# A long convolution's complex product by three real products in eight small tiles, and a new order of the operations ahead of the feed-forward loop

## The chip, the core and the metric

The kernel runs on one core of a Trainium2 chip. The core has five engines with a queue each: TensorE (PE, with its weight loads PEld), VectorE (DVE), ScalarE (ACT), GpSimd (POOL) and SyncE (SP), which here issues all DMAs. Each engine works through its instructions in the order of the program. The metric is the device time of one execution in microseconds, the median over the runs shown.

## The reference, cut to what matters

```python
x = A_q                                           # 1 x 2048 x 512
sa, ca, ga, sb, cb, gb = split(silu(c) @ w_mod)   # six vectors of 512
h = layernorm(x) * (1 + ca) + sa
kv = short_conv(k, shift_k) * v                   # 4 taps, causal, per channel
y = irfft(rfft(pad(kv)) * rfft(pad(ssm_k)))[:2048] + kv * ssm_D
x = x + ga * (h * y)
h = layernorm(x) * (1 + cb) + sb
x = x + gb * ((silu(h @ w_gate) * (h @ w_up)) @ w_down)   # 512 -> 1792 -> 512
```

Everything is float32. The long convolution has 2048 positions for each of 512 channels and is causal.

## The kernel before, in words

The kernel has a front part (modulation, short convolution, long convolution, first norm, gate, residual) and a feed-forward part over 28 sets, a set being one block of 128 of the 1792 hidden channels for one half of the 2048 rows. Here "row block" t = 0 to 3 is 512 rows; the first half of the sets works on row blocks 0 and 1.

**The long convolution** is a Fourier transform in two steps, done by matmuls, for four blocks `c_` of 128 channels. For the data: `load_k`, `load_v` (lines 115, 120), the taps on DVE (`tap0`, `tap`, lines 133, 141), the product with v (`times_v`, line 147), PE transposes (`x_turn`, line 167, tile `kvt`) and the first step (`x_first`, line 175, tile `s`, into `X[c_]`). For the kernel: `load_ssm` (line 723), `skip` (line 727, adds `ssm_D`), first step (`k_first`, line 195, also tile `s`), transposes back (`k_turn`, line 213, tile `kt`, into `K[c_]`). DVE then transposes 32x32 blocks of a quarter of `X[c_]`, a piece of 32 channels (`swap_x`, line 232, `STREAM_TRANSPOSE`).

The second step works on one piece n of 16. `second` (line 251) multiplies the 64 rows of the two halves `a` by a 64x64 matrix; its two column halves go to two halves of PSUM's partitions, so a call is four matmuls in the four 64x64 tiles of the array, 512 columns each. `x2nd` (line 262) does this for the data (tile `px`) and ACT copies the result to `xs`. `product` (line 266) does it twice for the kernel (tile `pk`), with the matrices `W2` and `W2S`, and DVE multiplies each with `xs` into `R`: four real products of real and imaginary parts, as two of doubled height. `inv` (line 275) goes back with `V1` and `V2` (tile `iv`), eight matmuls in 64x64 tiles, and ACT copies into `X`. `loop` (line 285) runs the pieces: `product(n)`, `x2nd(n + 1)`, `swap_x(n + 2)`, the hooks of n, `inv(n - 1)`, the hooks of `(n,)`. The other work of the front is hung on the hooks (from line 801 on): taps and first steps of later blocks, modulation (`mod_load`, `mod_part`, `mod_bc`, tiles `wm`, `pb`, `bcs`), loads, statistics (`do_stats`), gates (`do_gate`, `gate`, line 394: four ACT steps and two POOL steps for each row block).

The result of blocks 0 to 2 is put to DRAM and got back in another order (`put`, `get`, lines 238, 242, one and four DMAs); block 3 is swapped again by DVE. `y_pe` (line 403, tile `y`) does the last step, `y_gate` (line 415) multiplies with the gate `S1`, `add_c` and `add_y` (lines 795, 425) add to `xt`, with the statistics of the second norm (`bnb`, `mvb`, `rsb`).

**The feed-forward part** splits each float32 operand into a high and a low part in a reduced float32 type, and takes three matmuls for a product (`op_hi`, `op_lo`, `split_w`, `w8_hi`, `w8_lo`). Sets 0 and 1 are done plainly (`gu_pe`, line 621, tile `g`, 96 matmuls in all), sets 2 to 27 by `gate_up` (line 658), with seven products in the order 1, 5, 7, 2, 3, 6, 4 in place of eight. `split_w` (line 533) needs four sums and two low parts on POOL for each set. `downs` multiplies back (tile `dn`). Behind each product stands a place where more work is hung (`AT`, line 962): among it `norm2b` and `half_t` (lines 436, 470), the second norm and PE transposes (tile `nt`) of row blocks 2 and 3.

**What sets the order.** Every engine keeps the program's order, which is written out: first a list (lines 731 to 777), then `loop` with its hooks, then a list to the second set (lines 834 to 928), then the loop over sets. Tiles come from pools: `e8` has 8 buffers of 8 KB for each partition, `b16` 6 of 16 KB, `r4` 5 of 4 KB, PSUM in the front four double banks (`banks`). A tile is given out when an old one of its pool is no longer read.

Of the kernel before, what the change touches and what calls it, by code (L numbers as in the profile page):

```python
# [10 lines left out]
F32 = mybir.dt.float32  # L11
# [32 lines left out]
def adaln_h3_swiglu(ctx, tc, q, kT, vT, shk, ssm, dskip, wgu, wdn, c, wmod, e_fwd, e_inv, w_c, out):  # L44
# [122 lines left out]
    def x_turn(c_, half):  # L167

        pt = banks("kvt").rearrange("p a (j d) -> p (a j) d", j=4)
        for jj in range(8):  # L170
            pe.transpose(pt[:, jj], U[c_][:, 8 * half + jj :: J], ident)
        x = XT[c_, half] = r4([P, 8, P], F32, f"x{c_}{half}")
        act.copy(x, pt)
# [74 lines left out]
    xs, R = {}, {}  # L248
    PIECES = 4 * NB
# [16 lines left out]
    def product(n):

        R[n] = []
        for w in (W2, W2S):
            ps = second(w, K[n // 4], n % 4, "pk")  # L270
            r = r4([P, 2, 512], F32, "R")
            dve.tensor_tensor(r, ps, xs[n], op=ALU.mult)
            R[n].append(r)

    def inv(n):
        ps = banks("iv")
        for k, v in enumerate((V1, V2)):
            for a in range(2):
                for c_ in range(2):
                    pe.matmul(  # L280
                        ps[rows(a), c_, :], v[rows(c_)], R[n][k][rows(c_), a, :], start=(k == 0), stop=(k == 1)
                    )
        act.copy(piece(X[n // 4], n % 4), ps.rearrange("p g (k d) -> p (g k) d", k=16))

    def loop(hooks):
        for n in range(PIECES + 1):
            if n < PIECES:
                product(n)
            if n + 1 < PIECES:
                x2nd(n + 1)  # L290
            if n + 2 < PIECES:
                swap_x(n + 2)
            for f in hooks.get(n, ()):
                f()
            if n > 0:
                inv(n - 1)
            for f in hooks.get((n,), ()):
                f()
# [432 lines left out]
    load_k(0)  # L731
    load_e(0)
    load_e(1)
    load_ssm(0)
    load_e(2)
    load_e(3)
    load_v(0)
    load_k(1)
    load_v(1)
    wc = cp.tile([P, 4, 64], F32, name="wc")  # L740
    sp.dma_start(wc, w_c)
    W2, W2S, V1, V2 = (wc[:, i, :] for i in range(4))
    def kf(c_, *jqs):
        return [lambda jq=jq: k_first(c_, jq) for jq in jqs]

    def kt(c_, *ms):
        return [lambda m=m: k_turn(c_, m) for m in ms]

    def run(fs):
        for f in fs:  # L750
            f()

    tap0(0, dve)
    tap(0, 1)
    load_ssm(1)
    skip(0)
    run(kf(0, 0, 1, 2, 3))
    tap(0, 2)
    tap(0, 3)
    times_v(0, dve)  # L760
    x_turn(0, 0)
    x_turn(0, 1)
    x_first(0, 0)
    run(kt(0, 0, 1))
    x_first(0, 1)
    run(kt(0, 2, 3))
    tap0(1, dve)
    for t in range(1, KS):
        tap(1, t)
    load_k(2)  # L770
    swap_x(0)
    swap_x(1)
    x2nd(0)
    times_v(1, dve)
    load_v(2)
    tap0(2, act)
    skip(1)
# [17 lines left out]
    def add_c(t, *cs):
# [50 lines left out]
    rs = {0: norm2a(0, True)}
    w8_lo(0, pool)
    add_c(1, 0)
    y_now(1, 2, 3)
    mod_T(3)  # L850
    mod_T(4)
    y_pe(2, 0, 1)
    y_pe(3, 0, 1)
    y_pe(2, 2, 3)
    norm2b(0, rs[0], 0)
    norm2b(0, rs[0], 1)
    add_c(1, 1)
    norm_t(0, 0)
    norm_s(0, 0)
    y_gate(2, 0, 1)  # L860
    y_gate(3, 0, 1)
    add_y(2, 0, 4, (0, 1), pool)
# [204 lines left out]
```

## Time and profile before

| | before |
|---|---|
| median of 3 runs | 643.6 us (643.42 to 643.73) |
| the profiled execution | 643.63 us, span 641.9 us |
| PE, DVE, ACT, POOL busy | 601.9, 472.3, 299.5, 315.5 us |
| mean granted PE clock | 0.984 |
| first matmul of the feed-forward part | at 194.05 us |

All operations of the kernel are recorded through one helper, so they have one line (L40) in the profile, and groups are told apart by their tiles: `out<-in`, the program's names without buffer numbers. A group's row has engine, operation, tiles, shapes and count, then busy us, mean ns of one, and after the second bar the idle time ahead of it with what ended it. In order of time a row has start, length, engine, operation, count, and in brackets the idle time before it. Matmuls overlap, so the cost of a row of them is read from one start to the next.

### The profile page before, as it was taken

How to read it: one execution, taken by the hardware profiler on the slowest of the kernel's cores; microseconds unless marked ns; L12 is line 12 of the kernel's file. 1: busy time of each engine (PE TensorE's matmuls, PEld its weight loads, DVE VectorE, ACT ScalarE, POOL GpSimd, SP SyncE). 2: the span in 40 equal slices, each digit the busy share in tenths (PEclk: the TensorE clock that was granted, in tenths of full speed). 3: DMA queues.
4: the chain of work that ended last, by engine and by line, in shares of the span. 5: the costliest groups of instructions: out<-in, count | busy, mean ns of one | idle time of the engine just before them, and what ended most of it. 6: DMA issues, size and time to landing. Idle time of an engine off the chain costs nothing.

```text
span 641.9 us, 9081 instructions
## 1 busy us (share of the span) xinstructions
PE 601.9 (94%) x3604; PEld 454.8 (71%) x3604; DVE 472.3 (74%) x600; ACT 299.5 (47%) x439; POOL 315.5 (49%) x248
## 2 busy tenths in 40 slices
PE   2899999989697899999999999999999999999997
PEld 2756456534276788777778888878888888888885
DVE  5998767957978688877766886898565665656655
ACT  1867667874124545454544443544343333333320
POOL 0000000599254479775673767486565757575400
PEclk9999999989889999999999999999999999999999
DMA  8884492953931121302022111114210112120003
GB/s 293 370 300 161 165 234 86 269 103 137 242 115 66 34 67 33 99 33 67 20 79 66 34 34 65 34 66 154 75 67 34 65 38 86 43 65 1 0 2 131
DMA packets 30107, 64.68 MB, mean 101 GB/s; under 512 B 2289, under 2 KB 14705, under 8 KB 27506
## 3 DMA queue, kind: packets, MB, share of 16 engines
q1 hardware_dynamic: 30066, 64.11, 31.7%
q8 instruction: 28, 0.46, 0.3%
q14 instruction: 13, 0.11, 0.1%
HBM read 53.62 MB, written 10.49 MB: 100 GB/s over the span
## 4 chain that ended last, share of the span: by engine, by line
PE 54%; DVE 16%; ACT 5%; issue 2%; POOL 1%; ACTq 0%; DVEq 0%; POOLq 0%
PE dn L40 19%; PE b L40 9%; PE a L40 8%; PE c L40 8%; PE d L40 5%; DVE d L40 2%; DVE x L40 2%; PE y L40 2%; DVE acts L40 2%; DVE n L40 1%; DVE X L40 1%; ACT acts L40 1%; ACT op L40 1%; PE pk L40 1%; DVE c L40 1%
## 5 line engine op out<-in xcount | busy, mean ns | idle before, releaser
L40 PE MATMUL dn<-wd,acts 128*128 128x512 f32 x672 | 165.9, 390 | 0.5 <-DVE acts L40 0.5
L40 PEld LDWEIGHTS dn<-wd,acts 128*128 128x128 f32 x672 | 126.0, 188 | 27.9 <-DVE acts L40 1.1
L40 POOL TENSOR_TENSOR wa<-ws,wa 128x512 fp32r<-128x512 f32 (+1 forms) x52 | 60.6, 1188 | 110.9 <-ACT wa L40 103.1
L40 DVE TENSOR_TENSOR x<-x,dn 128x512 f32<-128x512 f32 x112 | 74.6, 680 | 54.4 <-PE dn L40 53.3
L40 PE MATMUL b<-op,wsum 128*128 128x512 f32 x312 | 79.7, 391 | 0.8 <-POOL wsum L40 0.8
L40 POOL TENSOR_TENSOR wsum<-sr,wsum 128x1024 fp32r<-128x1024 f32 x26 | 72.3, 2779 | 0.0
L40 PEld LDWEIGHTS b<-op,wsum 128*128 128x128 f32 x312 | 58.1, 188 | 13.3 <-POOL wsum L40 1.3
L40 POOL TENSOR_SCALAR rsa<-mva 128x4 f32<-128x4 f32 x8 | 2.5, 310 | 118.5 <-DVE mva L40 118.0
L40 PE MATMUL a<-op,wa 128*128 128x512 f32 x228 | 57.9, 389 | 0.0
L40 ACT ACTIVATE sg<-sg 128x512 f32<-128x512 f32 x26 | 16.5, 633 | 87.4 <-DVE sg L40 87.4
L40 DVE TENSOR_TENSOR R<-pk,xs 128x1024 f32<-128x1024 f32 x32 | 37.7, 1215 | 25.2 <-PE pk L40 25.2
L40 PEld LDWEIGHTS a<-op,wa 128*128 128x128 f32 x228 | 42.8, 188 | 8.9
L40 DVE STREAM_TRANSPOSE X<-X 128x1024 f32<-128x1024 f32 x20 | 45.3, 2277 | 0.1
L40 POOL TENSOR_TENSOR wd<-wds,wd 128x1024 fp32r<-128x1024 f32 x14 | 35.5, 2538 | 19.6 <-ACT wd L40 19.6
L40 ACT CAST acts<-d 128x512 fp32r<-128x512 f32 x26 | 15.3, 587 | 62.9 <-DVE d L40 36.5
L40 POOL TENSOR_TENSOR sr<-ws 128x256 f32<-128x256 f32 x52 | 43.1, 828 | 0.0
L40 PE MATMUL c<-op,wa 128*128 128x512 f32 x156 | 39.7, 390 | 0.0
L40 PE MATMUL d<-op,wsum 128*128 128x512 f32 x156 | 39.6, 389 | 0.0
L40 PE MATMUL c<-op,wsum 128*128 128x512 f32 x156 | 39.6, 389 | 0.0
L40 POOL TENSOR_TENSOR s<-s,bcs 128x2048 f32<-128x2048 f32 x8 | 36.5, 4568 | 0.3
L40 PE MATMUL pk<-K,wc 64*64 64x512 f32 x256 | 35.3, 626 | 1.1 <-ACT K L40 1.0
L40 DVE TENSOR_TENSOR op<-hraw,op 128x1024 fp32r<-128x1024 f32 x14 | 23.1, 1654 | 15.2 <-ACT op L40 15.2
(105 smaller groups left out, 1095.9 us busy)
## 6 DMA issues: line engine op xcount, KB each, us to landing
ws<-in_wgu SPq DMA_DIRECT2D x28, 512.0 KB, 3.3
wds<-in_wdn SPq DMA_DIRECT2D x14, 512.0 KB, 3.6
wm<-in_wmod SPq DMA_DIRECT2D x6, 1024.0 KB, 11.4
away<-X SPq DMA_DIRECT2D x3, 2048.0 KB, 7.5
X<-away SPq DMA_DIRECT2D x12, 512.0 KB, 11.2
kt<-in_kT SPq DMA_DIRECT2D x4, 1024.0 KB, 5.4
ss<-in_ssm SPq DMA_DIRECT2D x4, 1024.0 KB, 10.0
vt<-in_vT SPq DMA_DIRECT2D x4, 1024.0 KB, 10.1
```

The source lines that it names most:

```text
L40: return lambda *a, **k: self.tc.keep_in_program_order(f(*a, **k))
```

## The change

Three things change.

*The complex product.* Three real products are taken in place of four. `second` now takes pieces two at a time (64 channels; n runs over 8) and one of three 64x32 matrices m, and issues eight matmuls in 64x32 tiles. `x3` does the data side (three times for a pair of pieces, copied by ACT), `product3` the kernel side and DVE's product, in place. `inv3` goes back with three 32x64 matrices in 32x64 tiles: 24 matmuls into two PSUM tiles. The constants are made to fit.

*The order.* `loop` and its hooks are gone. One written list holds all operations from the first load to the end of sets 0 and 1. Steps are cut finer for it: the loads of block 0's `ssm` in quarters, `times_v` in four parts, the gate's ACT and POOL steps apart (`gate_n`, `gate_p`), statistics in halves. Four groups of six `warm` matmuls on an identity stand in it (before: one of four). The norm and transposes of row block 1 now stand ahead of the first `gu_pe`.

*Inside the loop over sets,* `half_t` moves from behind product 2 to behind product 3, and one `norm_stats` from 3 to 2.

```diff
-    def second(w, t, i, name):
+    def groups():
+        for i in range(2):
+            for c_ in range(2):
+                for a in range(2):
+                    yield i, c_, a, slice(64 * i + 32 * c_, 64 * i + 32 * c_ + 32)
+
+    def second(w, t, n, m, name):
         ps = banks(name)
-        for c_ in range(2):
-            for a in range(2):
-                pe.matmul(
-                    ps[rows(c_), a, :], w[rows(a)], piece(t, i)[rows(a), 16 * c_ : 16 * c_ + 16], start=True, stop=True
-                )
+        for i, c_, a, r in groups():
+            x = piece(t, 2 * (n % 2) + i)[rows(a), 16 * c_ : 16 * c_ + 16]
+            pe.matmul(ps[r, a, :], w[rows(a), m], x, start=True, stop=True)
         return ps
...
+    def x3(n, m):
+        if m == 0:
+            t = fp.tile([P, 2, 512], F32, tag="xs", name="xs", bufs=2)
+        else:
+            t = r4([P, 2, 512], F32, "xs")
+        xs[n, m] = t
+        act.copy(t, second(WX, X[n // 2], n, m, "px"))
+
+    def product3(n, m):
+        t = xs[n, m]
+        dve.tensor_tensor(t, second(WK, K[n // 2], n, m, "pk"), t, op=ALU.mult)
+
+    def inv3(n):
+        ps = [banks("iv") for _ in range(2)]
+        for m in range(3):
+            for i, c_, a, r in groups():
+                pe.matmul(ps[i][rows(a), c_, :], WV[r, m], xs[n, m][r, a, :], start=(m == 0), stop=(m == 2))
+        for i in range(2):
+            act.copy(piece(X[n // 2], 2 * (n % 2) + i), ps[i].rearrange("p g (k d) -> p (g k) d", k=16))
...
-    loop({
-        0: [lambda: tap(2, 1), lambda: load_ssm(2), lambda: x_turn(1, 0)],
...
-    })
...
+    load_k(0)
+    tap0(0, dve)
+    tap(0, 1)
+    load_ssm(0, 0)
+    load_ssm(0, 2)
+    load_ssm(0, 3)
+    warm(6)
+    load_e(2)
+    skip(0)
+    warm(6)
+    load_e(0)
+    k_first(0, 2)
...
+    x3(0, 0)
+    x3(0, 1)
+    mod_load(0, 5)
+    x3(0, 2)
+    product3(0, 0)
+    tap(2, 2)
+    x_first(1, 0)
+    load_ssm(3)
+    x3(1, 0)
+    load_x(0)
+    product3(0, 1)
+    x3(1, 1)
+    product3(0, 2)
+    product3(1, 0)
+    product3(1, 1)
+    k_turn(1, 2)
+    tap(2, 3)
...
+    x3(5, 0)
+    gate_p(0)
...
+    get(1)
+    product3(5, 2)
+    inv3(4)
+    inv3(5)
+    swap_x(13)
...
+    y_pe(0, 0, 1)
     load_w(0)
+    y_gate(0, 0, 1)
...
+    put(2)
+    mod_load(3, 4)
+    y_pe(2, 0, 1)
...
+    inv3(7)
+    w8_hi(0)
+    mod_part(4)
+    swap_x(14)
+    warm(6)
+    swap_x(15)
+    mod_part(3)
+    get(2)
+    y_pe(0, 2)
     load_w(1)
     load_wd(0)
...
+    norm_t(1, 1)
+    load_w(2)
     room()
+    op_lo("B21")
+    norm_s(1, 1)
+    gu_pe(1, 0, 0)
...
-        (5, 2): lambda: half_t(2, 0),
+        (5, 3): lambda: half_t(2, 0),
...
-        (6, 2): lambda: half_t(2, 1),
-        (6, 3): lambda: norm_stats(3, range(0, 2)),
+        (6, 3): lambda: half_t(2, 1),
+        (6, 2): lambda: norm_stats(3, range(0, 2)),
...
-        (7, 2): lambda: half_t(3, 0),
+        (7, 3): lambda: half_t(3, 0),
...
-        (8, 2): lambda: half_t(3, 1),
+        (8, 3): lambda: half_t(3, 1),
...
+    re, im = np.concatenate([co, -si]), np.concatenate([si, co])
+    w_k = np.concatenate([re, im - re, re + im], 1)
+    w_x = np.concatenate([re + im, re, im], 1)
+    w_v = np.concatenate([co + si, co - si, si, co, -co, si], 1)
```

More of the change, by code (lines that the diff above doesn't have):

```diff
@@ L170, in x_turn @@
         for jj in range(8):
-            pe.transpose(pt[:, jj], U[c_][:, 8 * half + jj :: J], ident)
+            pe.transpose(pt[:, jj], kv[c_][1][:, 8 * half + jj :: J], ident)
         x = XT[c_, half] = r4([P, 8, P], F32, f"x{c_}{half}")
@@ L266, in product @@
[L266 to L298, printed above, removed]
+    xs = {}
+    def groups():
+        for i in range(2):
+            for c_ in range(2):
+                for a in range(2):
+                    yield i, c_, a, slice(64 * i + 32 * c_, 64 * i + 32 * c_ + 32)
@@ L729, in skip, with load_wc @@
         dve.tensor_tensor(t, t, dsk[:, c_ * P : (c_ + 1) * P], op=ALU.add)
[L731 to L777, printed above, removed]
+    wc = cp.tile([P, 384], F32, name="wc")
+    WK, WX = (wc[:, 96 * i : 96 * i + 96].rearrange("p (m k) -> p m k", m=3) for i in range(2))
+    WV = wc[:, 192:].rearrange("p (m k) -> p m k", m=3)
+    def load_wc():
+        sp.dma_start(wc, w_c)
     def mod_mix():
@@ new lines, in adaln_h3_swiglu @@
+    tap(0, 2)
+    load_v(0)
+    k_first(0, 0)
+    load_e(3)
+    load_e(1)
+    k_first(0, 3)
+    load_ssm(0, 1)
+    load_k(1)
+    load_v(1)
+    k_first(0, 1)
+    load_k(2)
+    tap(0, 3)
+    times_v(0, 0)
+    times_v(0, 1)
+    x_turn(0, 0)
+    load_ssm(1)
+    load_wc()
+    k_turn(0, 0)
+    k_turn(0, 1)
+    times_v(0, 3)
+    mod_load(1, 2)
+    times_v(0, 2)
+    x_turn(0, 1)
+    k_turn(0, 2)
+    tap0(1, dve)
+    k_turn(0, 3)
+    tap(1, 1)
+    tap(1, 2)
+    tap(1, 3)
+    times_v(1, 0)
@@ new lines, in adaln_h3_swiglu @@
+    x_first(0, 0)
+    x_first(0, 1)
+    skip(1)
+    k_first(1, 3)
+    k_first(1, 2)
+    k_first(1, 0)
+    times_v(1, 1)
+    k_first(1, 1)
+    times_v(1, 3)
+    times_v(1, 2)
+    x_turn(1, 1)
+    mod_part(1)
+    swap_x(1)
+    swap_x(0)
+    k_turn(1, 0)
+    x_turn(1, 0)
+    k_turn(1, 3)
+    swap_x(2)
+    load_k(3)
+    load_v(2)
+    mod_bc(1)
+    swap_x(3)
+    tap0(2, act)
+    mod_part(2)
+    load_ssm(2)
+    tap(2, 1)
+    x3(0, 0)
+    x3(0, 1)
+    mod_load(0, 5)
+    x3(0, 2)
@@ new lines, in adaln_h3_swiglu @@
+    product3(0, 0)
[11 more added lines that the diff above has]
+    tap(2, 3)
+    k_turn(1, 1)
+    skip(3)
+    x3(1, 2)
+    x_first(1, 1)
+    do_stats(0, 0)
+    tap0(3, act)
+    product3(1, 2)
+    inv3(0)
+    times_v(2, 0)
+    times_v(2, 1)
+    inv3(1)
+    x_turn(2, 0)
+    times_v(2, 2)
+    times_v(2, 3)
+    x_turn(2, 1)
+    skip(2)
@@ new lines, in adaln_h3_swiglu @@
+    load_v(3)
+    k_first(2, 0)
+    k_first(2, 1)
+    tap(3, 1)
+    put(0)
+    swap_x(5)
+    swap_x(4)
+    k_first(2, 3)
+    swap_x(7)
+    mod_part(0)
+    k_first(2, 2)
+    x_first(2, 0)
+    x_first(2, 1)
+    tap(3, 2)
+    tap(3, 3)
+    times_v(3, 0)
+    k_turn(2, 0)
+    k_turn(2, 2)
+    k_turn(2, 1)
+    times_v(3, 2)
+    swap_x(6)
+    times_v(3, 1)
+    mod_bc(2)
+    x3(2, 0)
+    times_v(3, 3)
+    x3(2, 1)
+    product3(2, 0)
+    load_x(1)
+    load_x(2)
+    x3(2, 2)
@@ new lines, in adaln_h3_swiglu @@
+    product3(2, 1)
+    product3(2, 2)
+    x3(3, 0)
+    mod_bc(0)
+    do_stats(0, 1)
+    product3(3, 0)
+    load_x(3)
+    x3(3, 1)
+    product3(3, 1)
+    do_stats(3, 0)
+    x3(3, 2)
+    product3(3, 2)
+    gate_n(0, 0)
+    x_turn(3, 1)
+    gate_n(0, 1)
+    inv3(2)
+    swap_x(11)
+    swap_x(9)
+    get(0)
+    inv3(3)
+    put(1)
+    mod_part(5)
+    k_turn(2, 3)
+    x_turn(3, 0)
+    mod_bc(5)
+    swap_x(8)
+    do_stats(2, 0)
+    k_first(3, 1)
+    mod_mix()
+    k_first(3, 2)
@@ new lines, in adaln_h3_swiglu @@
+    swap_x(10)
+    k_first(3, 3)
+    k_first(3, 0)
+    do_stats(1, 0)
+    x3(4, 0)
+    product3(4, 0)
+    x3(4, 1)
+    x_first(3, 0)
+    x_first(3, 1)
+    x3(4, 2)
+    x3(5, 0)
+    gate_p(0)
+    do_stats(1, 1)
+    do_stats(2, 1)
+    x3(5, 1)
+    x3(5, 2)
+    do_stats(3, 1)
+    gate_n(1, 0)
+    gate_n(2, 0)
+    swap_x(14)
+    load_einv()
+    product3(4, 1)
+    product3(4, 2)
+    product3(5, 0)
+    product3(5, 1)
+    gate_n(1, 1)
+    gate_n(2, 1)
+    get(1)
+    product3(5, 2)
@@ new lines, in adaln_h3_swiglu @@
+    inv3(4)
+    inv3(5)
+    swap_x(13)
+    k_turn(3, 0)
+    k_turn(3, 3)
+    swap_x(15)
+    swap_x(12)
+    gate_n(3, 0)
+    y_pe(0, 0, 1)
+    load_w(0)
+    y_gate(0, 0, 1)
+    k_turn(3, 1)
+    add_c(0, 0)
+    add_c(0, 1)
+    k_turn(3, 2)
+    x3(6, 0)
+    x3(6, 1)
+    x3(6, 2)
+    gate_p(1)
+    product3(6, 0)
+    product3(6, 1)
+    product3(6, 2)
+    y_pe(1, 0, 1)
+    y_gate(1, 0, 1)
+    add_c(1, 0)
+    x3(7, 0)
+    add_c(1, 1)
+    inv3(6)
+    x3(7, 1)
+    gate_n(3, 1)
@@ L845, in adaln_h3_swiglu @@
+    y_gate(0, 3)
     add_c(0, 3)
[L846 to L849, printed above, removed]
+    w8_hi(1)
+    y_pe(1, 2, 3)
+    do_norm2a(0)
+    mod_T(4)
+    y_gate(1, 2, 3)
+    add_c(1, 2)
     mod_T(3)
[L851 to L852 removed]
     y_pe(3, 0, 1)
[L854 removed]
+    norm2b(0, rs[0], 1)
+    warm(6)
     norm2b(0, rs[0], 0)
[L856 to L857 removed]
     norm_t(0, 0)
     norm_s(0, 0)
[L860 to L862 removed]
```

233 lines of the change are left out of this document (112 added, 121 removed).

## The prediction

> **What bounds the kernel now.** I read the page first, then the busy time by stretches, then what DVE and PE waited for, and last the instructions in order of time. The page's head, slices and chain:
>
> ```profile
> span 641.9 us, 9081 instructions
> ...
> PE   2899999989697899999999999999999999999997
> ...
> PEclk9999999989889999999999999999999999999999
> ...
> PE 54%; DVE 16%; ACT 5%; issue 2%; POOL 1%; ACTq 0%; DVEq 0%; POOLq 0%
> ```
>
> The profiled execution took 643.63 us for a span of 641.9, so 1.7 lie around the span; the median shown is 643.6, the same. From slice 14 on PE is full at full clock. Before it the bound changes, as the busy time by stretches shows (columns: PE, PEld, DVE, ACT, POOL, clock, DMA share, GB/s):
>
> ```profile
> 7.67:57.72 50.05, 42.63 (x462) 30.26 (x463) 48.39 (x35) 32.14 (x40) 0.00 (x0) 1.00 0.84 330
> 57.72:112.75 55.03, 54.02 (x508) 29.16 (x506) 39.91 (x38) 38.36 (x46) 0.00 (x0) 1.00 0.55 148
> ...
> 7.67:194.05 186.38, 168.29 (x1688) 98.93 (x1688) 152.34 (x166) 112.31 (x139) 52.72 (x31) 0.95 0.68 207
> 194.05:216.51 22.46, 17.13 (x78) 13.71 (x76) 17.40 (x25) 12.19 (x17) 7.65 (x7) 0.92 0.17 59
> 216.51:641.90 425.39, 416.44 (x1841) 342.19 (x1841) 301.50 (x403) 173.48 (x283) 254.48 (x205) 1.00 0.17 55
> ```
>
> 7.67 is DVE's first tap, 194.05 the first matmul of the feed-forward part (`g`). To 57.72 DVE is full, then to 112.75 PE is. Over 7.67 to 194.05 DVE stands idle 34.0 us (186.38 - 152.34), mostly for `pk`:
>
> ```profile
> DVE R L40 <- PE pk L40: 25.2, 11, 6.6
> ```
>
> One turn of the loop in the middle stretch, in order of time:
>
> ```profile
> 74.55 1.95 PE L40 MATMUL pk<-K,wc 64*64 64x512 f32 x16
> 76.32 1.04 PE L40 MATMUL px<-X,wc 64*64 64x512 f32 x8
> 77.28 1.98 PE L40 MATMUL pb<-part,sel 128*128 128x512 f32 x4
> 79.20 1.95 PE L40 MATMUL iv<-R,wc 64*64 64x512 f32 x16
> 81.08 2.06 PE L40 MATMUL s<-x,er 64*128 64x128 f32 x32
> 83.06 1.06 PE L40 MATMUL pb<-wm,csb 128*32 128x512 f32 x8
> 84.06 1.95 PE L40 MATMUL pk<-K,wc 64*64 64x512 f32 x16
> ```
>
> PE has no gap in these 9.51 us; DVE waits because the next `pk` stands behind work of other blocks. So a stretch full on DVE is followed by one full on PE: what order and amount of the work cost is read here.
>
> **The cut.** Everything from the first `g` on I take as one block. Before, it is 641.9 - 194.05 = 447.9 us. Its own losses: 51 `g` matmuls took 22.46 us up to 216.51. A group of six takes 1.36 us by the starts below, so 51 need 11.6: 10.9 lost. One wait for POOL costs 259.19 - 256.82 - 1.36 = 1.0, and four waits for `n` cost 4.0:
>
> ```profile
> PE nt L40 <- DVE n L40: 4.0, 4, 1.2
> ```
>
> ```profile
> 255.46 1.52 PE L40 MATMUL c<-op,wa 128*128 128x512 f32 x6
> 256.82 1.52 PE L40 MATMUL a<-op,wa 128*128 128x512 f32 x6
> 259.19 1.66 PE L40 MATMUL b<-op,wsum 128*128 128x512 f32 x6 [0.84 <-POOL wsum L40]
> ```
>
> Without them the block is 432.0 us.
>
> **half_t one product later** (behind 3, not 2). Each time PE reaches the transposes 0.8 to 1.2 us before `n` is there; one product ahead of them is 1.36 us. Gain 4.0, bounds 0 and 4.0; I take 3.9. `hraw`'s copies come 1.36 later, and their reader is sets away.
>
> **The first sets in the new order.** Both row blocks are now normalised before the first `g`, and 96 `g` (21.8 us) and four downs (24 matmuls, 5.4) stand in one row. Of the 10.9 I take all as gone, since it was PE waiting on `op`, `n` and `sg` inside the group. What could bring it back is POOL, which has from the first weight split to the sums of the fifth set (f = 4):
>
> ```profile
> L40 POOL TENSOR_TENSOR s<-s,bcs 128x2048 f32<-128x2048 f32 x8 | 36.5, 4568 | 0.3
> L40 POOL TENSOR_TENSOR x<-x,s 128x1024 f32<-128x1024 f32 x4 | 9.9, 2488 | 3.6 <-DVE s L40 3.6
> L40 POOL TENSOR_TENSOR wd<-wds,wd 128x1024 fp32r<-128x1024 f32 x3 | 8.2, 2728 | 8.0 <-ACT wd L40 8.0
> L40 POOL TENSOR_TENSOR wsum<-sr,wsum 128x1024 fp32r<-128x1024 f32 x3 | 8.2, 2720 | 0.0
> L40 POOL TENSOR_TENSOR sr<-ws 128x256 f32<-128x256 f32 x6 | 5.4, 898 | 0.0
> L40 POOL TENSOR_TENSOR wa<-ws,wa 128x512 fp32r<-128x512 f32 x3 | 4.9, 1640 | 7.2 <-ACT wa L40 7.2
> L40 POOL TENSOR_TENSOR wg<-ws,wg 128x1024 fp32r<-128x1024 f32 x2 | 4.9, 2427 | 4.0 <-ACT wg L40 3.9
> ```
>
> 4.9 + 9.9 + 2 x 2.7 + three splits of about 9.6 (four sums of about 0.95, `wa` 1.6 and 1.4, `wsum` 2.7) = 49, against PE's 21.8 + 5.4 + two sets 19.0 + four downs 5.4 + 1.4 = 53. It just hides; if POOL starts late, each us late is paid. The gates' eight steps (36.5) come before, from `x3(5, 0)` on, and end under some 45 us of DVE work (eleven products, nine swaps, gates and adds) that stands between there and their last reader. I take 2 us of stalls for the whole block (0 to 6). Block after: 434.
>
> **The convolution.** Counted from the functions, a float32 matmul call being two instructions (four calls are x8 above): before, 256 `pk`, 128 `px`, 256 `iv` = 640 instructions in rounds of four tiles, 160 rounds. After, 24 `px` and 24 `pk` groups of 16 and eight `iv` groups of 48 = 1152 instructions of 512 columns, which, eight tiles at a time, are 144 rounds. A round of four, by the weight loads of the same `iv`:
>
> ```profile
> 79.68 0.15 PEld L40 LDWEIGHTS iv<-R,wc 64*64 64x64 f32 x4 [0.28 <-issue]
> ...
> 80.11 0.15 PEld L40 LDWEIGHTS iv<-R,wc 64*64 64x64 f32 x4 [0.28 <-issue]
> ```
>
> 0.43 us, so 68.8 before. The trace has no round of eight. Lower bound 0.43 (the `pb` 128*32 group fills the array with four tiles in one round too, 8 in 1.00); upper 0.86, if only four run at once. What also matters is how fast instructions follow each other, 0.054 us being needed. The fastest long row:
>
> ```profile
> 184.87 5.46 PE L40 MATMUL y<-X,ei 128*64 128x128 f32 x96
> 190.26 1.97 PE L40 MATMUL nt<-ident,n 128*128 128x128 f32 x16
> ```
>
> 5.39/96 = 0.056 each, with two tiles at once. I take this, as nearest: a round 0.45, 144 rounds 64.8 us, 4.0 less than before. [...]
>
> DVE: 32 products become 24 of the same size; ACT: 16 copies become 24. The rest that matters for DVE is what is moved ahead of the first `g`:
>
> ```profile
> L40 DVE TENSOR_TENSOR R<-pk,xs 128x1024 f32<-128x1024 f32 x32 | 37.7, 1215 | 25.2 <-PE pk L40 25.2
> L40 DVE BATCH_NORM_STATS2 bnb<-x 128x6 f32<-128x128 f32 x24 | 5.2, 281 | 0.2
> L40 DVE TENSOR_TENSOR x<-x,s 128x512 f32<-128x512 f32 x6 | 4.0, 670 | 0.1
> ...
> L40 ACT COPY xs<-px 128x1024 f32<-128x1024 f32 x16 | 16.2, 1013 | 26.3 <-PE px L40 19.1 <-issue 6.9 <-ACT kt L40 0.3
> ```
>
> 8 x 1.215 = 9.7 off DVE. 7.0 on: adds (2 x 0.67) and statistics (8 x 0.22) of row block 1, its aggregation, two halves of `n`, two low parts of `op` (1.2 each). DVE's sum: 152.3 - 9.7 + 7.0 = 149.6, so the first `g` can't be before 7.67 + 149.6 = 157. ACT gets 8.1 on 112.3 and stays under three quarters.
>
> **PE's sum to the first `g`**, from start to start: `s` 512 x 0.062 = 31.7, `kt` and `kvt` 192 x 0.124 = 23.8 (a 128x128 transpose, as the 16 `nt` in 1.97), `y` 256 x 0.056 = 14.4, `pb` 8.8, `pm` and 16 `nt` 4.0, the convolution 68.8 and 5.0 for changes of tile shape (16 turns; `px` 0.96 against two rounds 0.86, `iv` 1.88 against 1.72) = 156.5 before. It had 181.7 (12.31 to 194.05), so 25.2 were lost. After: 82.7 + 64.8 + 5.0 + 2.0 (the second block's `nt`) + 3.0 (half of the 24 `warm`, 24 instructions of the `nt` shape; the others fall into the wait for the first loads) = 157.4. `k_first(0, 2)` needs only the first 2 MB of loads and no DVE step. The first MB is there at 7.67, the second 3.2 later at the 330 GB/s of that stretch: 10.9, not 12.31 (by the work above, which began there). So PE allows 168, DVE 157. DVE's own start holds: `v` 0 lies behind 2.25 MB more, 14.5, and is wanted at 16.3 (taps 1.3 + 3 x 2.35, `skip` 0.3); `k` 1 comes at 19.8 against 18.8, 1 us that is part of what is kept lost below.
>
> **The order.** What of the 25.2 stays? The rows for it:
>
> ```profile
> 172.87 1.97 PE L40 MATMUL y<-X,ei 128*64 128x128 f32 x16 [3.93 <-DMA X<-away]
> ```
>
> ```profile
> away<-X SPq DMA_DIRECT2D x3, 2048.0 KB, 7.5
> X<-away SPq DMA_DIRECT2D x12, 512.0 KB, 11.2
> ```
>
> ```profile
> L40 DVE STREAM_TRANSPOSE X<-X 128x1024 f32<-128x1024 f32 x20 | 45.3, 2277 | 0.1
> ```
>
> Some 7 were slow clock (an estimate from such rows): here sixteen `y` take 1.97, twice the 0.056 each above, in a slice of clock 8 or 9; the new `warm` groups stand near it. 3.9 were `y` waiting for `X` from DRAM. `mod_load(3, 4)` now stands ahead of `get(2)` in SP's queue: 2 MB, 6.4 us at 330 GB/s; behind it wait `load_w(1)` and `load_wd(0)`. `put`, this and `get` are 7.5 + 6.4 + 11.2 = 25 us, while between `inv3(5)` and `y_pe(0, 2)` DVE has 33 us of work (seven swaps 16, six products 7, three gates 4, four adds with statistics 6). Hidden; uncovered it would cost the 3.9 again. Of the 14 left I keep 10: two engines near full that read each other lose something at each hand-over, and the wait from row block 1's statistics to `op` now lies ahead of the first `g` (pool steps 2, `n` 1, `op` 1.2, so about 4). First `g` at 168 + 10 = 178.
>
> **Sum:** 178 + 434 + 1.7 = 613.7, say 614.
>
> **Rivals.**
> - *The order trades one wait for another:* PE loses 25 again. For it: each queue is served in order, and PSUM has four double tiles for all. Against: the loss was in named places. 168 + 25 + 436 = 629. Chance 0.18.
> - *It packs better:* 3 lost, 607. For it: ACT and POOL have room. Against: the `n` wait alone is 4. 0.11.
> - *Instruction rate:* 62 ns each, as the `s` rows have (1.98/32). 1152 x 0.062 = 71.4, 6.6 more than taken: 621. Against: `s` has full-width weights. 0.10.
> - *Slower:* narrow tiles run four at once, not eight. For it: no round of eight in the trace, and all groups show at most four. Against: `pb` serves four column strips, `s` two row strips at full rate. A round is then 0.86, 144 rounds 123.8, 59 us more: 673. It decides from a round of about 0.66 us (30/144 above 0.45), five tiles at once. 0.09.
>
> **Numbers.** The forecast keeps 0.52: 614. About 1.3 us (0.2%) can be told from no change here. All cases but the last are faster by far more: faster 0.90, within 0.2% 0.01, slower 0.09. Range 602 to 632: it holds nearly all of the forecast and of the rate rival, half of the better packing and two thirds of the trade.
>
> **What would show it.** Weight loads of `px`, `pk`, `iv` in eights 0.43 to 0.46 apart; DVE's wait for `pk` under 12 us; first `g` at 170 to 186 with its 96 in about 22; no wait of `nt` for `n` behind set 3; the clock above 0.95 from 140 to 195. It is wrong if the eights come 0.6 or more apart, if the first `g` is past 192, or if POOL holds PE by over 6 us in the first sets.

## The result and the profile after

The changed kernel takes 613.5 us (median of 4 runs, 612.5 to 614.0) against 643.5 before on the same chip: a ratio of 0.953, 95% interval 0.9515 to 0.9548. The forecast was 614.0. Two single runs, one of a later experiment's kernel and one of the kernel before beside it, were slow ones (over one and a half times as long as the others) and are left out of all medians here. The profiled execution has a span of 611.8 us, 30.1 shorter than before. Slices and chain of its page:

```profile
PE   6999999979979999999999999999999999999997
...
PE 83%; DVE 10%; issue 2%; ACT 2%; POOL 1%; DMA 1%; SPq 1%; DVEq 0%; ACTq 0%; POOLq 0%
```

The chain of work that ended last was 54% PE and is now 83%; DVE's share fell from 16 to 10%. PE is full from slice 1 on (counted from 0), but for slices 8 and 11 and the last. The busy time by stretches (columns as before: PE, PEld, DVE, ACT, POOL, clock, DMA share, GB/s), cut where the first `g` now stands:

```profile
57.70:112.75 55.05, 55.05 (x846) 32.44 (x837) 51.97 (x58) 48.38 (x63) 15.34 (x17) 1.00 0.89 239
...
7.65:179.18 171.53, 159.88 (x2240) 103.52 (x2241) 162.99 (x174) 122.42 (x154) 55.09 (x36) 0.95 0.75 227
```

The first `g` moved from 194.05 to 179.18: 14.9 of the 30.1 us. From it to the end it is 611.8 - 179.2 = 432.6 us, not 447.9: the other 15.2. In the middle stretch PE (55.05 of 55.05) and DVE (51.97) are now both nearly full, where DVE had 39.91 before. DVE's idle time up to the first `g` fell from 34.0 to 8.5 us (171.53 - 162.99). The waits say the same (us in total, times, longest):

```profile
PE nt L40 <- DVE n L40: 2.3, 2, 2.0
...
DVE xs L40 <- PE pk L40: 2.3, 6, 0.5
```

DVE's wait for `pk` went from 25.2 to 2.3 us. The two waits of `nt` for `n` that are left stand ahead of the first `g`; the four behind set 3 are gone. What PE still loses is in a few rows, in order of time:

```profile
10.54 6.85 PE L40 MATMUL s<-er,ss 64*128 64x128 f32 x64 [3.93 <-DMA er<-in_e_fwd]
...
131.27 1.97 PE L40 MATMUL y<-X,ei 128*64 128x128 f32 x32
137.33 1.96 PE L40 MATMUL px<-X,wc 64*32 64x512 f32 x16 [4.10 <-DVE xs L40]
139.22 4.71 PE L40 MATMUL iv<-xs,wc 32*64 32x512 f32 x48
...
170.33 1.97 PE L40 MATMUL y<-X,ei 128*64 128x128 f32 x32 [0.71 <-ACT hraw L40]
173.46 0.33 PE L40 MATMUL nt<-ident,n 128*128 128x128 f32 x1 [1.16 <-ACT n L40]
174.07 0.44 PE L40 MATMUL nt<-ident,n 128*128 128x128 f32 x2 [0.28 <-DVE n L40]
176.55 2.76 PE L40 MATMUL nt<-ident,n 128*128 128x128 f32 x13 [2.05 <-DVE n L40]
179.18 22.73 PE L40 MATMUL g<-op,wg 128*128 128x512 f32 x96
201.75 5.60 PE L40 MATMUL dn<-wd,acts 128*128 128x512 f32 x24
```

The 96 `g` take 22.6 us (179.18 to 201.75) without a gap, and the downs follow. Ahead of them PE stops at 133.2 and goes on at 137.3. It loses 2.8 us in the first `s` (6.78 for 64, where 0.062 each makes 3.97), 4.1 waiting for the product `xs`, 2.9 behind that wait (`px` 1.89 and `iv` 4.65, where the same groups take 0.88 and 2.76 elsewhere), 4.2 in the four waits of the tail, and 1.0 in the last 13 `nt` (2.63, where 0.124 each makes 1.6): 15.0 in all. Where rows take about twice their usual time, the granted clock is low: 0.56 from 10.54 to 17.32, 0.59 from 137.33 to 143.87 and 0.56 from 176.55 to 179.18, against 1.00 from 144 to 175.

Why was `xs` late at 137, with DVE busy all along? DVE's instructions of the changed kernel in order of time:

```profile
125.41 4.88 DVE L40 TENSOR_TENSOR x<-x,s 128x512 f32<-128x512 f32 x1
...
131.12 4.13 DVE L40 TENSOR_TENSOR x<-x,s 128x512 f32<-128x512 f32 x1
...
140.71 0.69 DVE L40 TENSOR_TENSOR x<-x,s 128x512 f32<-128x512 f32 x1
...
171.46 5.03 DVE L40 TENSOR_SCALAR n<-x,rsb 128x512 f32<-128x512 f32 x2 [0.87 <-POOL rsb L40]
176.41 3.37 DVE L40 TENSOR_TENSOR op<-hraw,op 128x1024 fp32r<-128x1024 f32 x1
```

POOL's of the same stretches:

```profile
115.84 18.86 POOL L40 TENSOR_TENSOR s<-s,bcs 128x2048 f32<-128x2048 f32 x4 [2.28 <-ACT s L40]
148.21 9.29 POOL L40 TENSOR_TENSOR s<-s,bcs 128x2048 f32<-128x2048 f32 x2 [13.52 <-ACT s L40]
...
171.38 4.83 POOL L40 TENSOR_TENSOR wg<-ws,wg 128x1024 fp32r<-128x1024 f32 x2
176.17 5.87 POOL L40 TENSOR_TENSOR x<-x,s 128x1024 f32<-128x1024 f32 x2
```

The same add takes 4.88 and 4.13 us while POOL has its four gate steps of 4.7 us (115.84 to 134.70), and 0.69 at 140.71, in POOL's pause. Each of the two long adds ends 0.55 us behind the end of one of POOL's steps (the third from 125.14 to 129.75, the fourth to 134.70). Such an instruction, made longer while POOL is in a step, is called held below. `n` (two for 5.03) and `op` (3.37) lie beside POOL's `wg` and `x`. The products, with one input in PSUM, are not longer anywhere (1.21 on average, by the groups shown further down). The transposes aren't either (two for 4.49 at 154.31, beside POOL's steps from 148.21 to 157.50). Why just adds, `n` and `op` are held is not shown.

### The profile page after: what moved, and what is told of

It is laid out like the page before. It is cut to its first block, busy times and chain, and to the rows that moved or that the text cites. A ratio compares the mean times of both kernels' runs of the same rounds, so it can differ in the third digit from the quotient of the medians.

```text
span 611.8 us, 10197 instructions
## 1 busy us (share of the span) xinstructions
PE 593.1 (97%) x4156; PEld 460.9 (75%) x4156; DVE 479.5 (78%) x593; ACT 304.2 (50%) x447; POOL 318.6 (52%) x248
## 4 chain that ended last, share of the span: by engine, by line
PE 83%; DVE 10%; issue 2%; ACT 2%; POOL 1%; DMA 1%; SPq 1%; DVEq 0%; ACTq 0%; POOLq 0%
PE dn L40 23%; PE b L40 10%; PE a L40 10%; PE c L40 10%; PE s L40 5%; PE d L40 5%; PE g L40 4%; PE iv L40 3%; DVE x L40 3%; PE px L40 3%; PE pk L40 3%; PE kt L40 2%; PE pb L40 1%; PE kvt L40 1%; DVE bnb L40 1%
## 5 line engine op out<-in xcount | busy, mean ns | idle before, releaser
L40 POOL TENSOR_TENSOR sr<-ws 128x256 f32<-128x256 f32 x52 | 45.0, 866 | 0.0
L40 DVE TENSOR_TENSOR acts<-c,acts 128x512 fp32r<-128x512 f32 x26 | 18.0, 691 | 21.5 <-ACT acts L40 21.5
L40 PEld LDWEIGHTS c<-op,wa 128*128 128x128 f32 x156 | 29.2, 188 | 6.3 <-DVE op L40 0.3
L40 PEld LDWEIGHTS d<-op,wsum 128*128 128x128 f32 x156 | 29.3, 188 | 6.1
```

The lines of the kernel that those rows point to most:

```text
L40: return lambda *a, **k: self.tc.keep_in_program_order(f(*a, **k))
```

## The experiments

Every ratio is against the kernel before on the same chip (643.5 to 643.8 us). "After" is the changed kernel, 613.5.

**The products alone, in the old loop.** From the kernel before: `second`, `x3`, `product3`, `inv3` and the constants of the change; `loop` runs them for a pair of pieces in two turns, its hooks unchanged.

```diff
-                product(n)
...
+            p = n // 2
+            if n % 2:
+                product3(p, 2)
+            else:
+                if n < PIECES:
+                    product3(p, 0)
+                    product3(p, 1)
+                if n > 0:
+                    inv3(p - 1)
...
+            if n % 2 and n + 1 < PIECES:
+                for m in range(3):
+                    x3(p + 1, m)
```

> The kernel before with the three-product convolution alone, in the old loop: a pair of pieces has its three products in its two turns, x3 of the next pair at the end of the second turn, inv3 at the start of the turn after; everything else as before. Theory (the order brings most): 16 rounds of 0.43 us less on PE (6.9) and 9.7 us less on DVE, but each counts only in the stretches where that engine is full, so 643.5 goes to about 637 (632 to 641). Rival (the products bring most of the 30 us): 623 or less. Rival (they are no gain by themselves): 643 or more.

Measured 661.5 us, ratio 1.027 (1.025 to 1.029): 18 slower, not 6 to 7 faster. Its waits:

```profile
DVE xs L40 <- PE pk L40: 48.7, 14, 5.8
...
PE px L40 <- DVE X L40: 9.3, 7, 2.7
```

And its rows of PE in order of time, two turns of the loop:

```profile
72.92 1.95 PE L40 MATMUL pk<-K,wc 64*32 64x512 f32 x32
74.80 2.83 PE L40 MATMUL iv<-xs,wc 32*64 32x512 f32 x48
...
82.45 3.79 PE L40 MATMUL s<-x,er 64*128 64x128 f32 x32 [3.72 <-ACT x L40]
...
98.49 1.95 PE L40 MATMUL pk<-K,wc 64*32 64x512 f32 x32
```

The groups are as short as in the changed kernel, but two turns take 25.6 us (72.92 to 98.49); two of the old ones took 19. The loop runs in lock step: `pk` for three products comes in bursts, with `px` after its swaps, DVE waits 48.7 us for it (25.2 before), and PE waits for DVE and ACT in turn. So the smaller amount of work is worth nothing by itself in that order, at this pairing of the pieces. How much of the 18 us is the coarser turn, which the three products brought with them, is not separated; other pairings were not tried.

**`half_t` put back** behind product 2 (and `norm_stats` behind 3), the rest as after.

```diff
-        (5, 3): lambda: half_t(2, 0),
+        (5, 2): lambda: half_t(2, 0),
```

> The changed kernel with half_t behind product 2 again and that norm_stats behind 3. Theory: the four waits of nt for n are back, 4.0 us, so 613.5 goes to 617.4 (616.5 to 618). Rival (the wait would be taken up by other slack in the sets): 613.5 within 1.

Measured 617.9 us, ratio 0.960 (0.9586 to 0.9614): 4.3 more than after. PE's wait for `n` in this kernel's waits is back:

```profile
PE nt L40 <- DVE n L40: 6.3, 6, 2.0
```

6.3 - 2.3 = 4.0, the waits that were forecast.

**More work on PE, and more on DVE.** Neither leaves anything out; the same values are computed again. First: `px` of the pairs of pieces 0 to 3 twice, 24 rounds, 10.3 us of PE. Second: swaps 5 and 4 three times each (a block transposed thrice is transposed once), 9.1 us of DVE.

```diff
+        if n < 4:
+            for i, c_, a, r in groups():
+                ...
+                pe.matmul(ps[r, a, :], WX[rows(a), m], x, start=True, stop=True)
```

```diff
-    swap_x(5)
-    swap_x(4)
+    for _ in range(3):
+        swap_x(5)
+    for _ in range(3):
+        swap_x(4)
```

> The changed kernel with the px matmuls of pairs 0 to 3 issued twice into the same PSUM tile (same values): 12 groups of 16 at 0.86 us = 10.3 us more on PE between 38 and 87 us, nothing more on DVE or ACT. Theory (PE sets the pace of the front up to about 133 us): first g and end 9 to 11 later, about 623.5. Rival (DVE sets the pace, PE only looks full): 3 us or less, under 617.

> The changed kernel with two block transposes on DVE (pieces 4 and 5) done three times in place of once (same values): 4 more of 2.28 = 9.1 us on DVE near 61 us, nothing on PE. Theory (PE sets the pace, DVE is close behind with some 4 us of idle time between 61 and 133): 3 to 7 later, about 618.5. Rival (DVE has room, as its bound lies 10 us under PE's): 1 us or less. Rival (DVE is the bound): 9 later.

Measured: 623.3 (ratio 0.9684, 0.967 to 0.970), 9.8 more for 10.3 of PE, as expected; and 623.7 (0.9695, 0.9676 to 0.9714), 10.1 more for 9.1 of DVE, where 3 to 7 were expected. The second kernel's row of PE where the swaps were put:

```profile
86.97 1.96 PE L40 MATMUL px<-X,wc 64*32 64x512 f32 x16 [7.07 <-DVE xs L40]
```

PE waits 7.1 us for the products behind the swaps, and the two groups behind that wait run at about half speed (from start to start 1.89 for 16 `px`, where it is 0.86 at 91.68, and 1.94 for two `pb`, where it is 0.95 at 104.58), which is 2.0 of the 10.1. So PE took up some 2 us of the added DVE work and lost as much again in these slow rows. At these places no engine has room: each sets the pace within a few us of the other, and extra work on one of them costs about its own length.

**The adds out of POOL's way.** `gate_n(2, 1)`, ACT's half of the gate of row block 2, later, so that POOL's half of it (`gate_p(2)`) starts later and POOL pauses earlier, and both adds of row block 1 (`add_c(1, 0)`, `add_c(1, 1)`) from ahead of `inv3(6)` to behind the gate of row block 2.

```diff
-    gate_n(2, 1)
     get(1)
...
     gate_p(2)
     product3(7, 0)
     product3(7, 1)
     x3(7, 2)
+    gate_n(2, 1)
...
     y_gate(2, 0, 1)
+    add_c(1, 0)
+    add_c(1, 1)
```

> The changed kernel with the gates of POOL kept off DVE's adds: gate_n(2, 1) moved behind x3(6, 2), so that gate_p(2) starts some 5 us later, and add_c(1, 0), add_c(1, 1) moved behind y_gate(2, 0, 1). Theory (an add with both operands in SBUF is held while a POOL step on SBUF runs: 4.88 and 4.13 us at 125.4 and 131.1 in place of 0.69, and px waits 4.1 behind it): those adds take 0.7 again, px does not wait, the end is 7 earlier, 606.5 (604 to 609). Rival (PE sets the pace there and the adds' time is hidden): 613.5 within 1.5, the wait only moves.

Measured 615.9 (ratio 0.9566, 0.9549 to 0.9583), 2.4 more than after instead of 7 less. The edit did what it should at 125 and lost it later, as DVE's rows in order of time show:

```profile
125.33 0.69 DVE L40 TENSOR_TENSOR x<-x,s 128x512 f32<-128x512 f32 x1
...
147.02 4.10 DVE L40 TENSOR_TENSOR x<-x,s 128x512 f32<-128x512 f32 x1
```

PE's row behind them:

```profile
157.69 6.18 PE L40 MATMUL y<-X,ei 128*64 128x128 f32 x64 [5.04 <-DVE X L40]
```

The wait of 4.1 for `xs` is gone, but the moved add, now ahead of the last two swaps, was held by POOL's two steps for row block 3 (141.35 to 150.57 here, 148.21 to 157.50 after), and `y` waits 5.0 us for these swaps and then runs slow (6.18 for what takes 3.71 after).

**The tail out of POOL's way too.** On top of the last: the low parts of the first weights early on POOL (`w8_lo(0)`) or on DVE (`w8_lo(1)`), and POOL's `add_y(2, ...)` and `add_y(3, ...)` to behind `first_downs`.

```diff
+    w8_lo(0, pool)
...
+    w8_lo(1, dve)
...
-    w8_lo(1, pool)
...
-    w8_lo(0, pool)
...
-    add_y(2, 0, 4, (0, 1), pool)
...
-    add_y(3, 0, 4, (0, 1), pool)
...
+    add_y(2, 0, 4, (0, 1), pool)
+    add_y(3, 0, 4, (0, 1), pool)
```

> The kernel of e5, and in the tail POOL kept off DVE's n and op: w8_lo(0) right behind w8_hi(0), w8_lo(1) on DVE, the two POOL adds of blocks 2 and 3 behind wd_lo(0). Theory: n at 171.5 takes 1.0 in place of 5.0 and op_lo 1.2 in place of 3.4, less 1.2 for w8_lo on DVE: another 4 to 5 earlier than e5, about 602. Rival (POOL's work is now late in the first sets): wsum holds PE there and takes 2 or more of it back.

Measured 616.8 (ratio 0.9574, 0.9557 to 0.9592). The tail did get shorter; PE's rows in order of time show where the gain went:

```profile
160.65 5.15 PE L40 MATMUL y<-X,ei 128*64 128x128 f32 x64 [7.24 <-DVE X L40]
...
210.16 1.60 PE L40 MATMUL a<-op,wa 128*128 128x512 f32 x6 [1.57 <-DVE x L40]
```

Two `n` take 1.00 instead of 5.03, and from the swaps' end to the first `g` it is 19 us, 4 less than in the last kernel. But a weight step on POOL now holds one more add ahead of the swaps (1.93 at 153.65, beside POOL's `wg` of 2.79; `y` waits 7.2), and the moved adds make the first `a` wait for `x`. Both experiments moved POOL's long steps from one set of DVE instructions onto another; that the holds move with them is shown, their price only by the experiments with the late gate step below.

**The `warm` groups.** One kernel is after without all four; the other is the last kernel with 16 in place of 6 in the first two groups.

```diff
-    warm(6)
```

```diff
-    warm(6)
+    warm(16)
```

> The changed kernel without its four warm groups (48 matmul instructions). Theory: the two groups in the tail hold the clock; without them some of y, pm and nt from 155 on run at half clock, 2 to 4 later, 616; the two at the start do nothing, since PE still waits 3.9 behind them and the first s run slow anyhow (32 in 3.80). Rival (they only take PE's time): 613.5 or up to 1.5 less.

> The kernel of e6 with 16 in place of 6 matmuls in each of the two warm groups at the start, so that PE is busy until the first loads are there. Theory (the clock falls in the 3.9 us before the first s): the first 32 s take 2.0 in place of 3.8, the end is 1.5 to 2 earlier than e6. Rival (the last warm matmuls end after the loads and PE starts late, or DVE paces the start): the same as e6 or later.

Measured 613.5 (ratio 0.9526, 0.9511 to 0.9541) without them, the same as with them. The two groups of the tail filled waits: without them PE waits 1.80 us for the swaps (0.20 with them) and 0.94 for `n` (none with them), and the 64 `y` behind the first of these waits take 3.71 with and without them. With the longer ones it is 618.1 (0.9599, 0.9578 to 0.9621), 1.4 more than the kernel it was made from. PE's first rows of `s` in the kernel with the longer ones:

```profile
11.09 2.06 PE L40 MATMUL s<-er,ss 64*128 64x128 f32 x32
15.07 1.16 PE L40 MATMUL s<-er,ss 64*128 64x128 f32 x16 [1.92 <-issue]
```

The first 32 `s` do run at full speed here; the next ones wait 2.1 us, most of which the profile puts down to no releaser ("issue"), so what holds them stays open. All 64 are done at 18.4, 0.75 us earlier than in the kernel it was made from (19.2), and that gain is gone by 123.6. The 1.4 us are lost elsewhere: the 64 `y` behind the 7.2 us wait (at 160.6) take 6.58 here and 5.15 there. That the longer groups are the cause of this is not shown.

**One gate step later, alone.** From the changed kernel, `gate_n(2, 1)` behind `x3(7, 0)`, so that POOL's two steps for row block 2, which read its result, start later; the adds stay.

```diff
-    gate_n(2, 1)
     get(1)
...
     x3(7, 0)
+    gate_n(2, 1)
     add_c(1, 1)
```

> The changed kernel with one step moved: gate_n(2, 1) behind x3(7, 0), so that gate_p(2) starts only when the four adds of the first two blocks are done (e5 showed the adds free again at 0.69, but two of them stood ahead of swaps 14 and 15 there, PE idled 5.0 and its clock fell). Theory: the adds take 0.7, px(7, 0) has no 4.1 wait, swap 15 ends near 152.7 in place of 158.7, add_c(0, 2) is held some 2 by the last gate step; first g 4 earlier, end 609.5 (608 to 611). Rival (POOL's gates are only pushed onto the next adds): 613.5 within 1.5.

Measured 609.6 (ratio 0.9475, 0.946 to 0.949): 3.9 less than after, as expected. POOL's gate steps in it:

```profile
116.20 9.33 POOL L40 TENSOR_TENSOR s<-s,bcs 128x2048 f32<-128x2048 f32 x2 [2.79 <-ACT s L40]
137.60 18.51 POOL L40 TENSOR_TENSOR s<-s,bcs 128x2048 f32<-128x2048 f32 x4 [12.07 <-ACT s L40]
```

DVE's rows in order of time:

```profile
126.14 0.69 DVE L40 TENSOR_TENSOR x<-x,s 128x512 f32<-128x512 f32 x1
...
153.33 3.33 DVE L40 TENSOR_TENSOR x<-x,s 128x512 f32<-128x512 f32 x1
```

POOL does two of its steps, pauses for 12 us and does the other four under products and swaps, which aren't held (three products 3.52 at 141.12, two swaps 4.50 at 148.25). The adds that were held are short now, no wait of `px` for `xs` is left, and only one later add is held, behind the last swap. DVE is busy for 157.2 us up to the first `g`, 5.8 less than after; the first `g` comes 3.7 earlier, at 175.5. One moved line, an ACT step that POOL's steps wait for, with the same work on every engine, is worth 3.9 us: this is the run that shows the price of the hold. That ACT's copies come in another order is not the reason: in the changed kernel DVE had no wait from 125.41 to 143.8.

**The tail as well.** From the last kernel: `w8_lo(1)` and `w8_lo(0)` on DVE, between the norm's and `op`'s steps, and POOL's `add_y(2, ...)` ahead of the first `g`, behind a one-column POOL step that reads `op`'s low part, so that it starts only then.

```diff
+    w8_lo(1, dve)
...
-    w8_lo(1, pool)
     op_lo("B11")
+    w8_lo(0, dve)
+    pool.tensor_scalar(hold, BOP["B11"][:, 1, 0, 0:1].bitcast(F32), 1.0, None, op0=ALU.mult)
+    add_y(2, 0, 4, (0, 1), pool)
...
-    w8_lo(0, pool)
...
-    add_y(2, 0, 4, (0, 1), pool)
```

> The kernel of e9, and in the tail both w8_lo on DVE (right ahead of n of row block 1, and behind op_lo of B11), with a small POOL step that reads B11's low part ahead of POOL's add of row block 2, so that POOL reads nothing while n and op are made. Theory: n 1.0 in place of 5.0, op_lo 1.2 in place of 3.4, less 1.2 for w8_lo: 3.5 to 4 earlier than e9, about 606. Rival (as in e6 POOL or DVE are now late between the first g and set 4, dn, a and wsum wait): as e9 or later.

Measured 607.7 (ratio 0.9442, 0.9421 to 0.9462), 2.0 less than the last kernel and the fastest here: 5.9 under the changed kernel. DVE's rows of its tail:

```profile
166.38 1.21 DVE L40 TENSOR_TENSOR wg<-ws,wg 128x1024 fp32r<-128x1024 f32 x1
167.69 1.00 DVE L40 TENSOR_SCALAR n<-x,rsb 128x512 f32<-128x512 f32 x2
169.37 1.23 DVE L40 TENSOR_TENSOR op<-hraw,op 128x1024 fp32r<-128x1024 f32 x1 [0.68 <-ACT op L40]
...
175.47 2.09 DVE L40 TENSOR_TENSOR op<-hraw,op 128x1024 fp32r<-128x1024 f32 x1 [3.75 <-ACT op L40]
```

PE's row of the first `g`:

```profile
174.56 22.06 PE L40 MATMUL g<-op,wg 128*128 128x512 f32 x96 [0.66 <-ACT hraw L40]
```

The two `n` take 1.00, `op` 1.23, and PE's wait for `n` is gone (2.05 after, 1.03 in the last kernel). What it gives is less than the 3.5 to 4 expected: the holds on `n` (4.0 us) and on the first `op` (2.1) are gone, but 2.4 us of weight steps are now DVE's own, DVE waits 3.75 for ACT's part of `op`, and `g` waits 0.66 for ACT.

**The old amounts of work in the new order.** After, with 6.9 us more on PE (`px` twice for eight groups, 16 rounds) and 9.1 more on DVE (swaps 2 and 10 three times), about what the four products cost more; the values stay. The four products themselves were not tried in the new order.

```diff
+        if n in (0, 3) or (n == 5 and m < 2):
+            ...
-    swap_x(2)
+    for _ in range(3):
+        swap_x(2)
...
-    swap_x(10)
+    for _ in range(3):
+        swap_x(10)
```

> The changed kernel made to do what the old convolution costs PE and DVE in all: the px matmuls of pairs 0 and 3 and of two matrices of pair 5 issued twice (8 groups of 0.86 = 6.9 us on PE) and the block transposes of pieces 2 and 10 three times in place of once (4 of 2.28 = 9.1 us on DVE, against 9.7), same values. ACT keeps its 8 more copies. Theory (in the new order both engines set the pace, as e3 and e4 showed, each at its place): 10 to 16 later, 624 to 630, so that order and half_t alone are worth 14 to 19 of the 30 and the products the rest. Rival (the order is all): under 618. Rival (the products are all): over 636.

Measured 623.7 (ratio 0.9698, 0.9679 to 0.9716), 10.2 more than after and still 19.8 less than before. So with the amounts of before, the order and `half_t` give about 20 of the 30 us (`half_t` 4.3 of them), and the smaller amounts 10, where alone in the old loop they cost 18. The 16.0 us of extra work cost 10.2, about as much as 10.3 on PE or 9.1 on DVE alone did: work added to both engines at once is for the most part paid once. How the 10 depend on where the extra work was put was not tried.

## Why the prediction was right, point by point

**The first `g`: forecast 178, measured 179.2.** Two terms were off and nearly cancelled. PE began at 10.54 (10.9 forecast). The convolution's rounds: the weight loads of `iv` in eights,

```profile
55.19 0.18 PEld L40 LDWEIGHTS iv<-xs,wc 32*64 32x64 f32 x8 [0.25 <-issue]
55.62 0.18 PEld L40 LDWEIGHTS iv<-xs,wc 32*64 32x64 f32 x8 [0.25 <-issue]
```

come 0.43 apart, not 0.45: eight tiles do run at once, 144 rounds are 61.9 us, 2.9 under the term, and PE's work about 154.5. An instruction each 0.054 us: that settles the rivals of the instruction rate (621) and of four at a time (673). The lost time was taken as 10 and is 179.2 - 10.5 - 154.5 = 14.1; the rows above name 15.0, the same within the precision of the sum. The 4.2 of the tail were forecast in size ("about 4"), but 2.05 of them are the wait for the held `n`, which was not. The other 6 of the forecast were for hand-overs at no named place; 10.8 were lost at three: 2.8 in the slow start, 7.0 around the wait of `px`, 1.0 in the last `nt`. The 3.0 taken as PE's work for `warm` were no cost, since without these groups the time is the same.

**DVE's sum is the step that failed.** The total was right; this term of it was not. Forecast 149.6, so that DVE would allow 157 and have 11 us of room to PE's 168. Measured 163.0 busy, so it allows 170.7, later than PE's 10.5 + 154.5 = 165. The groups of after up to 200 (busy, mean ns):

```profile
L40 DVE TENSOR_TENSOR xs<-pk,xs 128x1024 f32<-128x1024 f32 x24 | 28.3, 1214 | 2.8 <-PE pk L40 2.3 <-ACT xs L40 0.5
L40 DVE TENSOR_TENSOR x<-x,s 128x512 f32<-128x512 f32 x8 | 13.1, 1642 | 0.2
```

The products cost what was forecast (1.21 each). The adds were priced by their row of before, 0.67; they took 1.64, 7.8 us more for eight. `n` took 4.0 more and `op` 2.1 (3.37 against 1.22), together 13.9. Two things stand against it in the gap of 13.4: 0.6 of this `op` lie behind the first `g`, and the second low part of `op` that the forecast counted (1.2) comes behind it too. So the held instructions make about 12 of the gap, and the other 1.3 are in no single row. The prediction set POOL's eight gate steps under DVE's work and asked only who reads their results; the new order puts them beside adds with two SBUF inputs, which they hold. In the kernel before the six adds of this stretch took 0.67 each, since they stood clear of POOL: all lie behind 163.9, and POOL's last gate steps end at 164.1:

```profile
145.67 18.42 POOL L40 TENSOR_TENSOR s<-s,bcs 128x2048 f32<-128x2048 f32 x4
```

But that kernel's trace did show the hold, further on, in the second pair of `n`. The group of `n` up to the first `g`, and the rows behind it in order of time:

```profile
L40 DVE TENSOR_SCALAR n<-x,rsb 128x512 f32<-128x512 f32 x2 | 1.0, 540 | 0.0
...
205.01 2.34 POOL L40 TENSOR_TENSOR x<-x,s 128x1024 f32<-128x1024 f32 x1
205.09 3.00 DVE L40 TENSOR_SCALAR n<-x,rsb 128x512 f32<-128x512 f32 x2 [0.27 <-POOL rsb L40]
```

Two `n` took 1.0 (from 185.05, with POOL idle but for the first 0.15 us) and 3.00 beside POOL's add. These two rows, compared, would have shown ahead of the change that DVE's price depends on what POOL does. The two runs with more work show that no room was left, and the orders with the late gate step and the clear tail that taking most of the holds away is worth 5.9 us.

**From the first `g` on: forecast 434, measured 432.6.** The 10.9 us of losses in the `g` group are gone as forecast, but for 0.8 (96 `g` in 22.6, where 21.8 was taken). `half_t` gives 4.3 (3.9 taken), and its waits come back as 4.0, the figure of before. The two us of stalls for POOL were too many: PE waits 0.3 for `wsum`, by its row in order of time.

```profile
233.49 1.65 PE L40 MATMUL b<-op,wsum 128*128 128x512 f32 x6 [0.30 <-POOL wsum L40]
```

**What was claimed of the clock is not borne out.** It should stay above 0.95 from 140 to 195, with the `warm` groups near; by stretches it is just under (0.84 before):

```profile
140.00:195.00 55.00, 50.49 (x523) 36.80 (x508) 51.36 (x68) 25.71 (x33) 29.27 (x18) 0.94 0.30 68
```

`px` and `iv` behind the wait at 133 and the last `nt` run at the low clock (0.59 and 0.56), and without any `warm` the clock is 0.93 from 112.75 to 180, as in the changed kernel from 112.75 to 179.18, and the time is the same. In the changed kernel these slow rows stand behind waits (`iv` 4.71 behind an idle 4.1, 2.8 elsewhere), and the slowness of `px` and `iv` goes with the wait: without the wait for `xs`, in the kernel with the late gate step, the same two groups take 1.09 and 2.83, and the clock is 0.97 from 7.65 to the first `g`, where it is 0.95 in the changed kernel. How long a wait it takes is not shown.

**The transfers** behind `mod_load(3, 4)` were hidden, as forecast: PE's row of the first `y` on what `get(2)` brings has no wait.

```profile
156.68 1.97 PE L40 MATMUL y<-X,ei 128*64 128x128 f32 x32
```

**The rivals.** "The order trades one wait for another" (629) didn't come: the `pk` wait is 2.3, where under 12 was asked. "It packs better" (607) didn't come either, but the order with the late gate step and the clear tail gets there (607.7), by the holds that it takes away. So the total was right with a wrong picture of DVE: 2.9 us too much for the convolution stood against 4 too little for the losses, and 1.2 too little up to the first `g` against 1.4 too much behind it. That it came within half a us is luck; that the new order is worth most of the 30 us is not.

## What to carry to other kernels

Less work on an engine that waits in lock step can give nothing, and coarser turns can cost: the three products, done for pairs of pieces, lost 18 us in the old loop, and in an order that kept both engines fed the smaller amounts of work were worth about 10 (by a stand-in for the old amounts). When POOL's long steps are moved, look not only at who reads their results but at which DVE instructions run beside them. Here adds (0.69 us alone, up to 4.88), `n` (two for 1.00, held 5.03) and `op` (1.22, held 3.37) were held, and products from PSUM (1.21) and transposes (2.3) were not: put such ones there instead. Where two engines are both near full, price a change on both sums, with the rows of the new neighbours rather than the old. One group's instructions that differ in length over the span are the sign to look for: the profile shows a hold as a longer instruction, not as a wait.

## What was not expected of the hardware

- An add of 0.69 us took up to 4.88, two norms of 1.00 took 5.03, while POOL was in a step of 2.4 to 4.7 us; products from PSUM (1.21) and transposes (2.3) beside the same steps kept their time. POOL's two steps for one row block, started later, are worth 3.9 us.
- Eight 64x32 or 32x64 tiles with float32 run a round of 512 columns in 0.43 us, as four 64x64 tiles do: 0.054 us for each instruction.
- `warm` matmuls in PE's pauses changed the rows' speed where they reached up to the next work (the first 32 `s` 2.06 us with the longer groups, where they take 3.79 in the changed kernel) and won no time: 613.5 with and without the four groups, and no gain with longer ones.
